# Attention, MoE and Sinkhorn MoE on one core: plain first block, four-quarter mixing, later column sums, an earlier check of decays, own room for raw pair inputs

## The chip, the cores and the metric

One Trainium2 chip, one core. The metric is the device time of one execution of the whole program, in microseconds (us).

## The reference

Three layers follow one another, all in fp32. The weights of the first MoE come as float64 words.

```python
f = 1.0 / (1.0 + np.exp(-f_logit))            # B 4, H 8, S 768, D 48
for t in range(S):
    state = f[:, :, t, :, None] * state + np.einsum('bhd,bhe->bhde', k[:, :, t], v[:, :, t])
    y[:, :, t] = np.einsum('bhd,bhde->bhe', q[:, :, t], state)
...
h = x @ w_in; r = np.maximum(h, 0.0); x = (r * r) @ w_out   # 3072 tokens, 384 -> 2048 -> 384
...
logits = x @ w_gate                                          # 8 experts
P = np.exp(logits - logits.max())
for _ in range(8):
    P /= P.sum(1, keepdims=True) + 1e-09
    P /= P.sum(0, keepdims=True) + 1e-09
    P *= N / E
for e in range(E):
    out += P[:, e:e + 1] * (np.maximum(x @ w1[e], 0.0) @ w2[e])   # 384 -> 1024 -> 384
```

## The kernel before, in words

**Order of the work.** Nothing is ordered by hand. `Plan` (from line 66) holds each piece of work as a step with an engine, an estimated length, a due time, the steps it needs and a lag (extra time until its result counts as there). `Plan.order` lists them as a list scheduler does, the step with the earliest due time first among those that are ready, and the program issues them in that list. On the chip each engine runs its instructions in that fixed order and waits where an input is not there: what is queued behind waits too.

**Attention.** The 3072 tokens are 24 chunks `c` of 128, six to a sequence. A chunk gets decays by scans on VectorE (`sg`, `minf` keeps the smallest), products of k and q with decays (`kq`), masked products among its tokens (`Psb`), and a state (`Sh`) from the chunks before it. `mix` (functions `new_y`, `mix_pair`, `mix`) makes y of a chunk on TensorE: four pairs p of heads, each head j of the pair in a half of y's partitions. Per pair there are two products with `Psb` (128 rows, 64 columns each, line 383) and, if the sequence has a state, two with the state (48 rows, 64 columns, line 386) into the same tile. Then `y_part` copies y as two rounded halves for the fast products: `hi` on ACT (step `yh`), the rest on VectorE (`yl`).

**First MoE.** Blocks `j` of 384 tokens (8 of them, three chunks each) by 16 weight tiles `f`; step i = 16 j + f. e1(i) (line 499) makes 9 products of 128x128 weights by 384 columns: for each third of the width w_hi x_hi, w_hi x_lo and w_lo x_hi. ACT makes relu, square and `hi`, VectorE `lo` (line 515), and e2(i) (line 525) 9 products into three accumulators. The weights are read as float64 words while the first block runs. A tile n goes through ACT (`cva`, `cvw`), VectorE (`cvb`: clamp line 937, fields 941, sign 945), POOL (`cvs`: sum, 949), then ACT (`cvh`: w_hi, line 280) and VectorE or POOL (`cvl`: w_lo, line 283). Which of the two, `LO_DVE` says: ten tiles on VectorE, six on POOL. e1(f) of the first block needs `cvl`(f). Attention chunks and these steps are interleaved by the plan. `keep_warm` (line 245) puts idle products of 128 columns on TensorE where the plan sees a gap near the start.

**Gates.** Logits `L` are collected, then 8 Sinkhorn iterations: row sums and scaling on VectorE (`skr`), column sums as a product with ones on TensorE (`skt`, line 989, tile `csum`), column scaling on VectorE (`skc`, from line 993). `pt` turns the result around. They run beside the first phases of the second MoE.

**Second MoE.** Three pairs p of 2 x 512 tokens, 8 experts; an e-phase is 66 products of 512 columns (line 678) for two steps, in products called p1, p2, p6, p5, p3, p7, p22, p4 that use sums of the inputs, and an o-phase is 72 products (line 729). ACT copies (line 696), VectorE adds (700, 705) and squares up hidden values (718), VectorE weighs o by the gate (752) and POOL accumulates (761). For each pair the inputs x are loaded (`ldx`, by SP's queue, in a ring `rawp` that the raw weights use too), summed (`xs`, VectorE) and split (`xhi` on ACT, `xlo` on VectorE). For p of 1 and 2 these wait for p4 of the step before, and p1 waits for all of them.

**Check of decays.** `in_range` takes the smallest decay of a row on VectorE and the maximum over partitions on POOL (`partition_all_reduce`, line 904); `choose` loads the flag into a register, and a slow path is taken after the program if it is set. The steps stand at `n1 + 200` and `n1 + 230` in the plan's time, in the second MoE.

## Time and profile before

| | us |
|---|---|
| time before, median of 3 runs (2130.74 to 2133.03) | 2131.81 |
| the profiled execution's own time | 2132.19 |
| its span in the trace | 2130.4 |
| TensorE busy | 2080.0 (98%) |
| VectorE busy | 1325.2 (62%) |
| ACT busy | 886.4 (42%) |
| POOL busy | 638.1 (30%) |

The span reaches from the first to the last instruction in the trace. Shares are of the span, over stages with different limits; the stages are read apart further down.

### The profile page before, as it was taken

How to read it: one execution, taken by the hardware profiler on the slowest of the kernel's cores; microseconds unless marked ns; L12 is line 12 of the kernel's file. 1: busy time of each engine (PE TensorE's matmuls, PEld its weight loads, DVE VectorE, ACT ScalarE, POOL GpSimd, SP SyncE). 2: the span in 40 equal slices, each digit the busy share in tenths (PEclk: the TensorE clock that was granted, in tenths of full speed). 3: DMA queues.
4: the chain of work that ended last, by engine and by line, in shares of the span. 5: the costliest groups of instructions: out<-in, count | busy, mean ns of one | idle time of the engine just before them, and what ended most of it. 6: DMA issues, size and time to landing. Idle time of an engine off the chain costs nothing.

```text
span 2130.4 us, 27837 instructions
## 1 busy us (share of the span) xinstructions
PE 2080.0 (98%) x10686; PEld 1762.8 (83%) x10686; DVE 1325.2 (62%) x2022; ACT 886.4 (42%) x1505; POOL 638.1 (30%) x636
## 2 busy tenths in 40 slices
PE   7889999999999999999999999999999999999998
PEld 5789899998987888878878888888887888888886
DVE  8973443332477666657677666756767766766674
ACT  4754444454643433423434433433433433443341
POOL 4531100010103333333332333334233243333331
PEclk9899999999999999999999999999999999999999
DMA  7342212110203111112122112121213111211210
GB/s 269 127 128 65 77 67 83 57 49 7 81 31 91 55 55 60 55 55 70 55 86 88 55 55 70 55 62 52 68 62 108 61 59 52 69 55 55 70 45 32
DMA packets 55114, 148.76 MB, mean 70 GB/s; under 512 B 6332, under 2 KB 15548, under 8 KB 54972
## 3 DMA queue, kind: packets, MB, share of 16 engines
q1 hardware_dynamic: 54972, 146.90, 21.6%
q8 instruction: 85, 1.39, 0.3%
q14 instruction: 57, 0.47, 0.1%
HBM read 135.28 MB, written 9.54 MB: 68 GB/s over the span
## 4 chain that ended last, share of the span: by engine, by line
PE 90%; DVE 6%; issue 1%; DMA 1%; POOL 1%; ACT 0%; SPq 0%; DVEq 0%; POOLq 0%; ACTq 0%
PE o L729 35%; PE e L678 33%; PE e L499 9%; PE a L525 8%; PE y L383 1%; PE y L386 1%; PE pp L344 1%; DVE cv_t L937 1%; DVE cv_t L945 1%; PE lg L540 1%; DVE lo L515 1%; PE ds L366 0%; DVE cv_t L941 0%; DVE w L283 0%; DVE sg L318 0%
## 5 line engine op out<-in xcount | busy, mean ns | idle before, releaser
L729 PE MATMUL o<-h,w 128*128 128x512 f32 x3456 | 792.8, 389 | 0.0
L729 PEld LDWEIGHTS o<-h,w 128*128 128x128 f32 x3456 | 648.1, 188 | 135.6 <-DVE sc L752 0.7
L678 PE MATMUL e<-x,w 128*128 128x512 f32 x3168 | 734.6, 391 | 10.4 <-DVE t L700 5.3
L678 PEld LDWEIGHTS e<-x,w 128*128 128x128 f32 x3168 | 597.2, 189 | 137.5 <-DVE t L700 7.0
L696 ACT COPY s<-e 128x512 f32<-128x512 f32 x288 | 168.9, 586 | 836.1 <-PE e L678 831.4
L761 POOL TENSOR_TENSOR acc<-acc,sc 128x512 f32<-128x512 f32 x258 | 334.4, 1303 | 536.4 <-DVE sc L752 529.5
L752 DVE TENSOR_TENSOR sc<-o,pb 128x512 f32<-128x512 f32 x264 | 182.0, 690 | 372.3 <-PE o L729 339.1
L718 DVE SCALAR_TENSOR_TENSOR h<-v,h 128x512 fp32r<-128x512 f32 x384 | 275.3, 736 | 1.8 <-ACT h L713 1.3
L713 ACT ACTIVATE h<-v 128x512 fp32r<-128x512 f32 x384 | 242.2, 631 | 52.8 <-DVE v L705 52.6
L705 DVE TENSOR_TENSOR v<-e,s 128x512 f32<-128x512 f32 x288 | 198.0, 688 | 74.7 <-ACT w L663 56.5
L650 POOL TENSOR_TENSOR rawa<-rawa 128x256 f32<-128x256 f32 x96 | 81.1, 845 | 537.4 <-DMA rawa<-in_wa_dram 347.8
L499 PE MATMUL e<-x,w 128*128 128x384 f32 x1152 | 229.0, 342 | 9.7 <-DVE w L283 6.2
L499 PEld LDWEIGHTS e<-x,w 128*128 128x128 f32 x1152 | 200.6, 190 | 16.7 <-DVE w L283 7.8
L515 DVE TENSOR_TENSOR lo<-g,hi 128x384 fp32r<-128x384 f32 x128 | 83.3, 653 | 208.6 <-ACT hi L511 208.6
L525 PE MATMUL a<-hi,w 128*128 128x384 f32 x768 | 200.1, 341 | 0.0
L667 DVE TENSOR_TENSOR w<-rawa,w 128x768 fp32r<-128x768 f32 x192 | 157.8, 823 | 8.1 <-ACT w L663 8.1
L663 ACT CAST w<-rawa 128x768 fp32r<-128x768 f32 x192 | 135.2, 728 | 29.6 <-DMA rawa<-in_wa_dram 12.4
L525 PE MATMUL a<-lo,w 128*128 128x384 f32 x384 | 131.0, 341 | 11.8 <-DVE lo L515 11.7
L525 PEld LDWEIGHTS a<-hi,w 128*128 128x128 f32 x768 | 140.3, 191 | 1.5 <-issue 0.3
L504 ACT ACTIVATE g<-e 128x384 f32<-128x384 f32 x128 | 62.9, 491 | 179.6 <-PE e L499 163.2
L328 POOL TENSOR_TENSOR kq<-kq,sg 128x512 f32<-128x512 f32 x24 | 30.9, 1287 | 290.7 <-DVE sg L318 161.6
L667 DVE TENSOR_TENSOR w<-rawc,w 128x768 fp32r<-128x768 f32 x96 | 92.5, 964 | 2.1 <-ACT w L663 2.0
(103 smaller groups left out, 1313.1 us busy)
## 6 DMA issues: line engine op xcount, KB each, us to landing
rawa<-in_wa_dram SPq DMA_DIRECT2D x96, 384.0 KB, 3.0
rawc<-in_wc_dram SPq DMA_DIRECT2D x96, 384.0 KB, 3.4
raw<-in_wm_dram SPq DMA_DIRECT2D x16, 768.0 KB, 6.2
pb<-ptd SPq DMA_DIRECT2D x24, 512.0 KB, 3.7
fraw<-in_fkq_dram SPq DMA_DIRECT2D x23, 512.0 KB, 4.0
...
```

The source lines that it names most:

```text
L499: pe.matmul(ps, w[:, wl, k * 128:(k + 1) * 128], xx[:, xl, k, :], start=n == 0, stop=n == 3 * KD - 1)
L525: pe.matmul(acc1[j][m], w[:, wl, D + m * 128:D + (m + 1) * 128], g, start=f == 0 and n == 0, stop=f == NF - 1 and n == 2)
L663: act.copy(out=W2[g, k][:, 0, 0:n], in_=src)
L667: dve.tensor_tensor(out=W2[g, k][:, 1, 0:n], in0=src, in1=W2[g, k][:, 0, 0:n].bitcast(F32), op=ALU.subtract)
L678: pe.matmul(ps, w[a], x[b], start=start and n == 0, stop=stop and n == 2, skip_group_check=True)
L696: act.copy(out=snap[g, n], in_=bank[g, "a"])
L705: dve.tensor_tensor(out=vs[g, k], in0=bank[g, k], in1=other, op=ALU.add)
L713: act.activation(out=hs[g // 2, t, f][:, 0], in_=vs[g, k], func=ACTF.Relu)
L718: dve.scalar_tensor_tensor(out=h[:, 1], in0=vs[g, k], scalar=0.0, in1=h[:, 0].bitcast(F32), op0=ALU.max, op1=ALU.subtract)
L729: pe.matmul(ob[q, t, m], w[:, a, c:c + 128], h[:, b], start=f == 0 and n == 0, stop=f == 3 and n == 2)
L752: dve.tensor_tensor(out=dst, in0=ob[q, t, m], in1=pbt[p, e][:, t * TB:(t + 1) * TB], op=ALU.mult)
L761: eng.tensor_tensor(out=acc[p, t, m], in0=acc[p, t, m], in1=sc[q, t, m], op=ALU.add)
```

## The change

- **Plain first block.** In block j = 0 e1 and e2 use plain fp32 products with the summed weight itself, tile `R`: three products for each of e1 and the three accumulators where there were nine. That block has no `hi`, no `lo` and no rounded halves of y. e1(f) needs `cvs`(f); `cvh` and `cvl` are due 16 steps later, all sixteen `cvl` on VectorE. The slots of `R` are used again for w tiles.
- **Quarters.** y of a chunk lies in two PSUM tiles, pair p in tile p % 2. Head j of pair p writes half j ^ (p & 1) of the partitions. Two pairs go together: their four products with `Psb`, then their four with the state. Weight rows are permuted in the host's layout to match. The copies of y are two instructions each; mix of a chunk needs `yl` of the chunk before.
- **Column sums.** The lag of `skr` is 2.8 instead of 0.8, so `skt` is listed later.
- **Check of decays.** It moves to `n1 - 12`, the last block of the first MoE, the flag's copy to POOL; `choose` needs the first o of super-step 14.
- **Raw inputs of pairs 1 and 2** get a pool of their own, are loaded earlier, summed and split earlier, each split behind the last product that reads its old tile; p1, p6 and p22 need only their own part.
- `dynamic_dma_scratch_size=1024` is set when the program is built.

```diff
-LO_DVE = (4, 6, 8, 9, 10, 11, 12, 13, 14, 15)
...
+    def cv_total(n):
+        R[n] = wb.tile([128, WCOL], F32, tag=f"b{n}", name="r")
+        F64(nc, cvt[n], raws[n]).total(R[n])
+
     def cv_hi(n):
-        act.copy(out=new_w(n)[:, 0, :], in_=cvt[n])
+        new_w(n)
+        act.copy(out=W[n][0], in_=R[n])

     def cv_lo(n):
-        (dve if n in LO_DVE else pool).tensor_tensor(out=W[n][:, 1, :], in0=cvt[n], in1=W[n][:, 0, :].bitcast(F32), op=ALU.subtract)
+        dve.tensor_tensor(out=W[n][1], in0=R[n], in1=W[n][0].bitcast(F32), op=ALU.subtract)
...
-        add(("cva", n), "act", 0.74, due, lambda n=n: cv_abs(n), [("ldw", n), if_(n >= 3, ("cvl", n - 3))], start=CV_AT + CV_STEP * n)
+        add(("cva", n), "act", 0.74, due, lambda n=n: cv_abs(n), [("ldw", n), if_(n >= 3, ("cvs", n - 3))], start=CV_AT + CV_STEP * n)
...
-        add(("cvh", n), "act", 0.74, due, lambda n=n: cv_hi(n), [("cvs", n), if_(n >= NF - 2, ("cvs", n - 4))])
-        add(("cvl", n), *(("dve", 0.88) if n in LO_DVE else ("pool", 1.78)), due, lambda n=n: cv_lo(n), [("cvh", n)])
+        add(("cvs", n), "pool", 1.9, due, lambda n=n: cv_total(n), [("cvb", n, 2), ("cvw", n)])
+        gone = [(s, k) for k in left_by(n) for s in ("e2", "cvl")] + ([("cvs", n - 4)] if n >= 14 else [])
+        add(("cvh", n), "act", 0.8, due + NF, lambda n=n: cv_hi(n), [("cvs", n)] + gone)
+        add(("cvl", n), "dve", 0.95, due + NF, lambda n=n: cv_lo(n), [("cvh", n)])
...
+    def y_at(c, p):
+        return tmp["y", c, p % 2], p // 2
+
+    def mix_in(c, p, rows=64):
+        vv, st = vt[c % 3], Sh.get(c)
+        y, n = y_at(c, p)
         for j in range(2):
-            h = 2 * p + j
-            pe.matmul(y[64 * j:64 * j + rows, p, :], vv[:, h * DH:h * DH + rows], Psb[c][:, j, p, :], start=True, stop=st is None)
...
+            h, o = 2 * p + j, 64 * (j ^ (p & 1))
+            pe.matmul(y[o:o + rows, n, :], vv[:, h * DH:h * DH + rows], Psb[c][:, j, p, :], start=True, stop=st is None)
+
+    def mix_state(c, p, rows=64):
+        kk, st = kq[c % 3], Sh.get(c)
+        y, n = y_at(c, p)
+        for j in range(2):
+            o = 64 * (j ^ (p & 1))
+            if st is not None:
+                pe.matmul(y[o:o + rows, n, :], st[64 * j:64 * j + DH, p, 0:rows], kk[64 * j:64 * j + DH, 1, p, :], start=False, stop=True)

     def mix(c):
         new_y(c)
-        for p in range(NP):
-            mix_pair(c, p)
+        for p in range(0, NP, 2):
+            for f in (mix_in, mix_state):
+                for i in range(2):
+                    f(c, p + i)
         Psb.pop(c)
...
+        if i < NF:
+            for k in range(KD):
+                pe.matmul(ps, R[i][:, k * 128:(k + 1) * 128], xx[:, 0, k, :], start=k == 0, stop=k == KD - 1)
+            return
...
+            if j == 0:
+                pe.matmul(acc1[j][m], R[f][:, D + m * 128:D + (m + 1) * 128], g, start=f == 0, stop=f == NF - 1)
+                continue
```

The lines on pairs, column sums and decays:

```diff
-        x2r[p, t] = rawp.tile([128, KD, TB], F32, tag="raw", name="xraw")
+        x2r[p, t] = pools["xr"].tile([128, KD, TB], F32, tag=f"x{t}", name="xraw") if p else rawp.tile([128, KD, TB], F32, tag="raw", name="xraw")
...
-            plan.load(("ldx", (p, t)), 786, u - 5.9 + 0.01 * t, lambda p=p, t=t: ldx(p, t),
-                      [("x2o", j, KD - 1) for j in js] + slot_of["x", (p, t)], n=len(js))
+            gone = slot_of["x", (0, t)] if p == 0 else ["right"] + [(s, p - 1, n) for s, n in (("xs", 3), ("xlo", 0), ("xlo", 1)) if p > 1]
+            plan.load(("ldx", (p, t)), 786, u - (9.0 if p else 5.9) + 0.01 * t, lambda p=p, t=t: ldx(p, t),
+                      [("x2o", j, KD - 1) for j in js] + gone, n=len(js))
         for n in range(4):
-            add(("xs", p, n), "dve", 0.69, u - 3.0 + 0.1 * n, lambda p=p, n=n: x_sum(p, n),
-                [("ldx", (p, 0)), ("ldx", (p, 1)), before, ("xs", p, n - 1) if n else None])
...
+            add(("xs", p, n), "dve", 0.69, u - (5.5 if p else 3.0) + 0.1 * n, lambda p=p, n=n: x_sum(p, n),
+                [("ldx", (p, 0)), ("ldx", (p, 1)), "left", ("xs", p, n - 1) if n else ("xlo", p - 1, 2) if p else None])
+
+        for i, (n, k, old) in enumerate(((0, 3, "p3"), (2, 4, "p7"), (1, 2, "p4"))):
+            d = u - (4.5 if p else 3.0) + 0.3 * i
...
-            needs["p1"] += [("xlo", p, n) for n in range(3)]
+            for name, n in (("p1", 0), ("p6", 2), ("p22", 1)):
+                needs[name] += [("xlo", p, n)]
...
-        add(("skr", it), "dve", 1.7, d, lambda: sk.rows(P), [done], lag=0.8)
+        add(("skr", it), "dve", 1.7, d, lambda: sk.rows(P), [done], lag=2.8)
...
+    def in_range_all():
         pool.partition_all_reduce(gmx, mx, 128, bass.bass_isa.ReduceOp.max)
-        dve.tensor_copy(out=flag, in_=gmx)
+        pool.tensor_copy(out=flag, in_=gmx)
...
-    add("range", "dve", 1.0, n1 + 200, in_range, ["P", ("o", 10, 1, 2)])
-    add("choose", "dve", 0.1, n1 + 230, choose, ["range", ("o", 14, 1, 2)])
+    add("range", "dve", 0.3, n1 - 12, in_range, [("scanf", NCH - 1)])
+    add("rangeall", "pool", 3.5, n1 - 11, in_range_all, ["range"])
+    add("choose", "dve", 0.6, n1 + 100, choose, ["rangeall", ("o", 14, 0, 0)])
```

VectorE's queue at the end of the first block, before: `w` is a `cvl`, `Psb` the masking of a chunk, `sg` to `d` the scans of the next chunk, and the two `lo` belong to steps 14 and 15; the next `lo` in the queue, three rows on, is that of step 16.

```order
L349 TENSOR_TENSOR Psb<-pp,mask 128x512
L283 TENSOR_TENSOR w<-cv_t,w 128x768
L349 TENSOR_TENSOR Psb<-pp,mask 128x512
L515 TENSOR_TENSOR lo<-g,hi 128x384
L324 SCALAR_TENSOR_TENSOR sg_125<-sg_125,d_126 128x516
L325 TENSOR_TENSOR minf<-minf,sg_125 128x4
L316 MEMSET sg_124 128x8
L317 MEMSET d_126 128x4
L318 SCALAR_TENSOR_TENSOR sg_124<-sg_124,d_126 128x516
L319 TENSOR_SCALAR d_126<-sg_124 128x4
L320 RECIPROCAL d_126<-d_126 128x4
L515 TENSOR_TENSOR lo<-g,hi 128x384
```

The same place with the change, from behind the last sign to the `lo` of step 16:

```order
L340 SCALAR_TENSOR_TENSOR sg_125<-sg_125,d_126 128x516
L341 TENSOR_TENSOR minf<-minf,sg_125 128x4
L298 TENSOR_TENSOR w<-r,w 128x768 x4
L332 MEMSET sg_124 128x8
L333 MEMSET d_126 128x4
L334 SCALAR_TENSOR_TENSOR sg_124<-sg_124,d_126 128x516
L335 TENSOR_SCALAR d_126<-sg_124 128x4
L336 RECIPROCAL d_126<-d_126 128x4
L340 SCALAR_TENSOR_TENSOR sg_124<-sg_124,d_126 128x516
L341 TENSOR_TENSOR minf<-minf,sg_124 128x4
L298 TENSOR_TENSOR w<-r,w 128x768 x5
L560 TENSOR_TENSOR lo<-g,hi 128x384
```

The `lo` of steps 14 and 15 are gone, nine `cvl` stand where one stood (a tenth a little earlier), and `Psb` comes behind the `lo` of step 16.

TensorE's queue at the mix of the last chunk, before: `a` are accumulators of the first MoE, `vt` the values, `kq` the queries; the last two rows stand there four times in all, once for each pair.

```order
L525 MATMUL a1_4404<-hi_4685,w_805 128x384 x2
L525 MATMUL a1_4404<-lo_4686,w_805 128x384
L525 MATMUL a2_4405<-hi_4685,w_805 128x384 x2
L525 MATMUL a2_4405<-lo_4686,w_805 128x384
L383 MATMUL y_4743<-Psb_4688,vt2_129 64x128 x2
L386 MATMUL y_4743<-kq2_123,Sh_4623 64x128 x2
```

The same mix with the change; the last four rows stand there twice:

```order
L573 MATMUL a2_4216<-lo_4503,w_799 128x384
L408 MATMUL y_4560<-Psb_4505,vt2_129 64x128 x2
L408 MATMUL y_4561<-Psb_4505,vt2_129 64x128 x2
L416 MATMUL y_4560<-kq2_123,Sh_4438 64x128 x2
L416 MATMUL y_4561<-kq2_123,Sh_4438 64x128 x2
```

The products with `Psb` of two pairs now stand together, and behind them the four with the state, into two tiles y.

TensorE's queue in the e-phase beside the Sinkhorn iterations, before: `csum` is a column sum, the e rows are products of the second MoE.

```order
L989 MATMUL csum<-sk_cs,sk_ones 128x8
L678 MATMUL e_5812<-x_5131,w_5341 128x512 x3
L678 MATMUL e_5812<-x_5131,w_5312 128x512 x3
L678 MATMUL e_5828<-x_5130,w_5406 128x512 x3
L678 MATMUL e_5832<-x_5130,w_5406 128x512 x6
L678 MATMUL e_5828<-x_5132,w_5583 128x512 x3
L989 MATMUL csum<-sk_cs,sk_ones 128x8
L678 MATMUL e_5852<-x_5132,w_5583 128x512 x3
L678 MATMUL e_5862<-x_5132,w_5406 128x512 x3
L678 MATMUL e_5862<-x_5130,w_5406 128x512 x3
L678 MATMUL e_5828<-x_5132,w_5583 128x512 x3
L989 MATMUL csum<-sk_cs,sk_ones 128x8 x2
```

Between two column sums with the change:

```order
L1047 MATMUL csum<-sk_cs,sk_ones 128x8
L730 MATMUL e_5599<-x_5040,w_5132 128x512 x3
L730 MATMUL e_5637<-x_5040,w_5145 128x512 x3
L730 MATMUL e_5637<-x_5040,w_5132 128x512 x3
L730 MATMUL e_5651<-x_4969,w_5268 128x512 x3
L730 MATMUL e_5655<-x_4969,w_5268 128x512 x6
L730 MATMUL e_5651<-x_4999,w_5412 128x512 x3
L730 MATMUL e_5674<-x_4999,w_5412 128x512 x3
L730 MATMUL e_5681<-x_4999,w_5268 128x512 x3
L730 MATMUL e_5681<-x_4969,w_5268 128x512 x3
L1047 MATMUL csum<-sk_cs,sk_ones 128x8
```

Where 18 and 12 products stood between column sums, 30 stand now.

## Rows read from the trace of the kernel before

**Rows 1.** Busy time by stretch: stretch, length, PE, PEld, DVE, ACT, POOL, PEclk, DMA, GB/s.

```profile
50.00:60.00 10.00, 6.97 (x43) 6.22 (x44) 9.86 (x15) 6.91 (x11) 5.52 (x3) 0.50 0.47 158
34.00:143.65 109.65, 86.80 (x541) 74.80 (x540) 106.45 (x127) 66.76 (x108) 60.70 (x35) 0.89 0.44 142
144.00:594.00 450.00, 449.90 (x3230) 416.67 (x3229) 172.80 (x321) 222.96 (x414) 45.12 (x39) 1.00 0.19 62
```

**Rows 2.** The chain that ended last: start, length, work; second MoE.

```profile
626.30 2.05 PE e L678 x9
...
652.59 16.65 PE o L729 x72
...
934.44 16.34 PE o L729 x72
...
971.04 16.38 PE o L729 x72
...
1131.10 16.32 PE o L729 x72
1147.42 14.96 PE e L678 x66
```

**Rows 3.** Timeline of DVE: start, length, engine, line, operation; two conversions.

```profile
59.73 0.55 DVE L937 TENSOR_SCALAR cv_t<-cv_t 128x768 f32<-128x768 f32 x1
...
61.78 0.95 DVE L283 TENSOR_TENSOR w<-cv_t,w 128x768 fp32r<-128x768 f32 x1
62.65 2.20 DVE L937 TENSOR_SCALAR cv_t<-cv_t 128x768 f32<-128x768 f32 x1
...
67.23 2.21 DVE L937 TENSOR_SCALAR cv_t<-cv_t 128x768 f32<-128x768 f32 x1
```

**Rows 4.** Timeline of POOL beside them; in brackets the idle time before.

```profile
61.99 2.44 POOL L949 TENSOR_TENSOR cv_t<-cv_t,raw 128x768 int32<-128x768 int32 x1 [2.60 <-issue]
64.39 1.51 POOL L331 TENSOR_TENSOR kq<-kq,sg 128x512 f32<-128x512 f32 x1
```

**Rows 5.** Timeline of DVE: the last sign, and lo of step 16.

```profile
126.11 0.96 DVE L945 SCALAR_TENSOR_TENSOR cv_t<-raw,cv_t 128x768 int32<-128x768 int32 x1
...
140.81 0.54 DVE L515 TENSOR_TENSOR lo<-g,hi 128x384 fp32r<-128x384 f32 x1
```

**Rows 6.** Timeline of PE: warm-up passes and what follows them.

```profile
37.54 2.62 PE L245 MATMUL warm<-shift 128*128 128x128 f32 x22
39.91 3.65 PE L499 MATMUL e<-x,w 128*128 128x384 f32 x18
```

**Rows 7.** Timeline of PE: the end of block 1; e1(18), then e2(16).

```profile
132.94 4.62 PE L499 MATMUL e<-x,w 128*128 128x384 f32 x16 [1.74 <-DVE w L283]
...
142.09 1.72 PE L499 MATMUL e<-x,w 128*128 128x384 f32 x9
143.65 0.51 PE L525 MATMUL a<-hi,w 128*128 128x384 f32 x2
```

**Rows 8.** Timeline of PE: the mix of chunk 7.

```profile
217.28 0.44 PE L383 MATMUL y<-Psb,vt 128*64 128x128 f32 x4
217.65 0.43 PE L386 MATMUL y<-kq,Sh 48*64 48x128 f32 x4
...
220.22 0.67 PE L366 MATMUL ds<-vt,Kn 128*64 128x48 f32 x16
```

**Rows 9.** Timeline of POOL: the reduction over partitions.

```profile
956.16 0.38 POOL L904 PARTITION_ALL_REDUCE gmx<-mx  x1 [5.96 <-issue]
```

**Rows 10.** Timeline of PE: start of the second pair.

```profile
1112.58 2.20 PE L678 MATMUL e<-x,w 128*128 128x512 f32 x9
1116.97 7.77 PE L678 MATMUL e<-x,w 128*128 128x512 f32 x33 [2.19 <-ACT s L696]
```

**Rows 11.** Timeline of PE: start of the third pair.

```profile
1616.73 2.20 PE L678 MATMUL e<-x,w 128*128 128x512 f32 x9
1621.25 14.83 PE L678 MATMUL e<-x,w 128*128 128x512 f32 x57 [2.32 <-ACT s L696]
```

125 lines of the change are left out of this document (69 added, 56 removed).

## The prediction

> **What bounds the kernel now.** I read the page first, then the busy time by stretches, then the chain of waits, and last the timelines of single engines where chain and stretches showed a loss. The profiled execution took 2132.19 us, 0.38 above the median of the runs shown (2131.81); the sum below is made against 2132.19. By the stretches [rows 1], TensorE is never idle in blocks 2 to 8 of the first MoE (144 to 594 us: 449.90 of 450), so there a removed pass of TensorE is worth its length. In block 1 (34 to 143.65) it is VectorE that is full: 106.45 of 109.65, with TensorE at 86.80. The reader should see that TensorE has 23 us to spare there, and that its clock was granted at 0.89 in that stretch and at 0.50 from 50 to 60, when the product waited for the conversion. The second MoE is a chain of e-phases and o-phases. An undisturbed e-phase lasts 14.96 [rows 2]; what a phase takes above that is loss.
>
> **Plain first block.** What VectorE does to convert a weight tile (clamp, fields, sign) takes 61.78 − 59.73 = 2.05 us when POOL is quiet; the next one, from 62.65 to 67.23, takes 4.58 [rows 3]. In between POOL ran two instructions, at 61.99 and 64.39 [rows 4]: so each of POOL's large elementwise instructions costs VectorE (4.58 − 2.05) / 2 = 1.26 us. A `cvl` costs VectorE 62.65 − 61.78 = 0.87 from start to start, though its own row says 0.95; a `lo` of 0.54 [rows 5] so costs about 0.48. Before the last sign of a conversion, which ends at 126.11 + 0.96 = 127.07 [rows 5], the change
> - removes 14 `lo`: 14 × 0.48 = 6.7;
> - takes 6 `cvl` off POOL: 6 × 1.26 = 7.6;
> - moves two of VectorE's eight `cvl` behind it: 2 × 0.87 = 1.7.
>
> The last sign then ends 16 us sooner, at 111. By the order ten `cvl` (8.7), two copies of x (about 1) and the scans of two chunks follow, and then `lo(16)`. Before, that `lo` came 140.81 − 127.07 = 13.7 behind the sign [rows 5]: scans, and two `cvl`, two `lo` and two `Psb`, each under 0.9: some 9.5 of it scans. So it comes at 111 + 8.7 + 1 + 9.5 = 130.2, and e2(16), which started at 143.65 [rows 7], behind it. TensorE has to be there by then. What plain products cost it: 22 warm-up passes of 128 columns lie between 37.54 and 39.91 [rows 6], 0.108 each, two passes to a product. A product of 384 columns is 6 × 0.108 = 0.646, a step of six products 3.88, where a step of 18 fast ones takes twice 143.65 − 142.09, or 3.12 [rows 7]: 16 × 0.76 = 12 us more. From 34 on TensorE then has 86.80 + 12, less 3 for the mixes of three chunks (below) and 3 for warm-ups that the order no longer has: 93, which ends at 127 if it never waits. The 23 us to spare so hide the 12; if the cover were smaller, TensorE would set the end. Before, its last wait was for the last `cvl`, up to 132.94 [rows 7]; now e1(15) needs the sum of its tile alone.
>
> VectorE's 130 and TensorE's 127 are close, so I take e2(16) at 130.6, **−13**. High end: 17 (127). Low end: 5, where the scans among the `cvl` are stretched by POOL and TensorE waits here and there for the first tiles. From ACT 16 `hi` go; it has 40 us to spare here.
>
> **Quarters.** The mix of one chunk is eight groups of four passes, from 217.28 to 220.22, 0.367 each [rows 8]. The two halves of a pair start together and take two passes and a switch: 0.367 = 2 × 0.108 + 0.151. The change puts two pairs side by side. The products with `Psb` (full height, half the columns) keep their number: four to a group, one switch, 4 × 0.108 + 0.151 = 0.58. The products with the state are 48 rows by 64 columns, a quarter of the array each. If the four quarters run at once, a group of eight instructions takes 0.367. A chunk is 2 × (0.58 + 0.367) = 1.89 instead of 2.94: 1.05 saved. If only two run at once the group takes 0.58 and the chunk 2.32: 0.62 saved. Of the chunks with a state, 15 lie where TensorE is never idle (7 to 11, 13 to 17, 19 to 23): 15.7 or 9.3 us. The trace shows two row halves at once (that pace), and never four quarters. The state's group already has both row halves at work [rows 8], so I take **−15.7** and keep 9.3 as the low end. The y copies become two instructions on ACT and VectorE where one was, and the next chunk's mix waits for y only through `yl`; both engines have half their time free [rows 1], so I price that at 0.
>
> The Trainium skill, "TensorEngine Tiling (Array Packing)", Restrictions and Gotchas, speaks against it: different row tiles cannot access the same PSUM bank simultaneously. In the old group as in the new one, both row halves of a pair write one y tile, and the old one ran at 0.367, not at 4 × 0.108 + 0.151. What the rule would give stands among the rivals.
>
> **Column sums later.** The e-phase that starts at 626.30 ends at 652.59: 26.29 us, 11.3 above 14.96 [rows 2]. Five column sums stand in it: TensorE reaches each before VectorE has the row sums, and queued behind are the e products, for which the next steps of VectorE wait. By the order three stay in it, and the rest follow later. If the loss went with the number, two fifths of 11.3 = 4.5 would go. But the chain of the eight iterations gets later by it, and the first o-phase's scaling needs the end of that chain: next late are the accumulators of o. I take **−2**, between 0 and 6.
>
> **Range of decays.** From the end of an o-phase at 934.44 + 16.34 = 950.78 to the next at 971.04 are 20.26 us [rows 2], 5.3 above 14.96. POOL's all-reduce stands there, with 5.96 us ahead of it in which POOL waits for nothing shown [rows 9]: no accumulation runs meanwhile, the buffers of o stay taken, and TensorE waits. The change puts it into the last block of the first MoE, where POOL is 10% busy [rows 1] and TensorE takes nothing from it: hidden. The flag's copy goes to POOL's queue, and only the late `choose` waits for it. I take **−5.3** (low end 4.0: `choose` still waits at a border).
>
> **Raw inputs of a pair.** At the second pair TensorE starts its first nine products at 1112.58, stands 2.19 us, and the o-phase begins at 1131.10: 18.52, so 3.6 lost [rows 2, 10]. At the third, 1616.73 to 1621.25 + 14.83 = 1636.08: 19.35, 4.4 lost, again with the halt after the first nine [rows 11]. VectorE and ACT make the sums and halves of x there, after the last p4, ahead of what p2 and p6 need. The change loads x nine of the plan's steps ahead (5.9 before) into room of its own (SP issues it; the weight loads queued behind it no longer share its slots), forms the sums 5.5 ahead, and each half behind the last product that used it; p1 waits for its own alone. Of 8.0 lost I take **−5.5**; one `xlo` of about 1 us still falls between VectorE's steps at each border. Ends: 1 and 7.8.
>
> **The sum.** 13 + 15.7 + 2 + 5.3 + 5.5 = 41.5; 2132.2 − 41.5 = **2090.7** us. All low ends together are 5 + 9.3 + 0 + 4 + 1 = 19.3 (2113), all high ones 17 + 15.7 + 6 + 5.3 + 7.8 = 51.8 (2080).
>
> **Rivals.**
> - Two quarters at a time: the mix saves 0.62, and the time is 2090.7 + 6.4 = 2097. For it: no row shows more than two at once. Against it: nothing in the pace of the old groups is taken by waiting.
> - Row halves of one bank take turns: a state group of eight passes, two columns at once, would be 8 × 0.108 + 0.151 = 1.0, a chunk 2 × (0.58 + 1.0) = 3.16, 0.22 more than now on 15 chunks: 2090.7 + 15.7 + 3.3 = 2109.7. Against it stand the old groups of 0.367 with both row halves in one y tile [rows 8].
> - The first block gains nothing, because the ten `cvl` with the scans between them now stand ahead of `lo(16)` and take what was freed: 2103.7.
> - Block 1 goes as fast as TensorE can, 17 us: 2086.7. It needs the scans and `cvl` to be quick once POOL is quiet.
> - **Slower**: plain products at half clock. The clock was 0.50 where TensorE stood waiting for the conversion [rows 1]. A step at half clock is 7.75; sixteen are 124, and the other work of TensorE up to 144 is about 86.80 − 16 × 3.12 = 37: from 34 on that ends at 195 instead of 143.65, 51 later. 2132.2 + 51 − 28.5 (the other four terms) = 2155. It decides once the plain steps run at 0.61 of full speed on the mean (34 + 62 / 0.61 + 37 is 29 above 143.65); the 0.89 of the whole stretch [rows 1], and waits that get shorter, speak against it.
> - That the conversion is not lightened can be excluded: the order shows the 16 `lo` gone from VectorE and six `cvl` from POOL.
>
> **Chances.** Forecast 0.56 (its own range 2083 to 2100), two quarters 0.15, block 1 as fast as TensorE 0.11, first block without gain 0.10, turns in a bank 0.05, half clock 0.03. I give 2078 to 2110 as the range: it leaves out the half clock, half of the turns in a bank, and tails of the others. About 0.2% (4.3 us) can be told from no change. Only the half clock is slower: 0.03; 0.02 lies within 0.2%, for several low ends with a new wait at a border; faster 0.95.
>
> **What would show it.** In the changed kernel e2(16) should start near 131, with VectorE still full to about 110, the conversion of a tile taking 2.05 us with POOL quiet, and a plain step 3.9. A mix of a late chunk should take 1.9 us (2.3: two quarters; above 2.9: turns), with the starts of all four state products within some ns. The all-reduce should stand in POOL before 594, no o-phase near 950 should follow an e-phase of 20, and the two pairs' e-phases should be near 16. The prediction is wrong if the e-phase with the column sums gets longer than 26.3, if TensorE now waits for `cvl` in block 2, or if the clock falls under 0.8 in block 1.

## The result, and the profile after

The changed kernel took 2105.14 us (median of 4 runs, 2102.58 to 2107.77), the kernel before 2132.42 beside it; the ratio is 0.9873, 95% interval 0.9856 to 0.9890. That is 27.3 us faster, where 41.5 were forecast: the time lies in the range, a good third of the gain is missing. The profiled execution took 2106.62 us, 25.6 less than the one of before.

First lines of the page of the changed kernel: the span, and busy time by engine.

```profile
span 2104.9 us, 27580 instructions
...
PE 2064.0 (98%) x10558; PEld 1734.1 (82%) x10558; DVE 1314.3 (62%) x2029; ACT 878.9 (42%) x1513; POOL 629.3 (30%) x631
```

TensorE works 16 us less, and the rest of the gain (25.5 us of span) is idle time that went. The program is a row of stages, so the difference can be read off one mark after the other. The marks are the start of e2(16), of the first and the fourth e-phase of the second MoE (e-phase 1 and 4), of e-phases 11, 15 and 34, all by the timeline of TensorE, and the last addition on VectorE.

| stretch | before | after | forecast | measured |
|---|---|---|---|---|
| start to e2(16): plain first block | 143.65 | 138.16 | −13 | −5.5 |
| to e-phase 1: mixes of blocks 2 to 8 | 443.71 | 428.54 | −15.7 | −15.2 |
| e-phase 1 to 4: column sums | 112.99 | 115.79 | −2 | +2.8 |
| 4 to 11: no change there | 218.96 | 218.96 | 0 | 0 |
| 11 to 15: range of decays | 130.50 | 125.15 | −5.3 | −5.35 |
| 15 to 34: both borders of pairs | 602.43 | 601.77 | −5.5 | −0.7 |
| 34 to the last addition, and from there to the end | 478.1 | 476.5 | 0 | −1.6 |

Busy time by stretch of the changed kernel (columns as in [rows 1]): two stretches ahead of block 1, block 1, a tenth of it, and the blocks where TensorE is full.

```profile
14.00:18.00 4.00, 4.00 (x20) 2.33 (x19) 3.83 (x9) 0.89 (x2) 0.00 (x0) 0.50 1.01 413
18.00:22.00 4.00, 4.00 (x27) 3.15 (x26) 0.82 (x3) 1.07 (x3) 1.19 (x1) 0.50 1.01 406
...
34.00:138.16 104.16, 89.58 (x452) 54.54 (x453) 99.13 (x122) 62.27 (x100) 52.08 (x30) 0.95 0.46 157
...
115.00:125.00 10.00, 6.49 (x17) 3.69 (x18) 9.85 (x12) 4.29 (x8) 6.47 (x5) 0.91 0.24 60
144.00:560.00 416.00, 416.00 (x3120) 393.47 (x3119) 170.99 (x332) 211.55 (x410) 45.89 (x38) 1.00 0.20 64
```

The plain products did not lose the clock: 0.95 over the block, against 0.89 [rows 1]. But TensorE still has 14.6 us idle there, 3.5 of it from 115 to 125, near the end. And ahead of the block, from 14 to 22 us, TensorE is busy without a gap at half clock, 1.2 GHz: experiment 3 shows what that was worth.

**Block 1.** The marks on VectorE came near where they were forecast, those on TensorE did not. Timeline of VectorE: the last sign (it ends at 111.86; forecast 111) and `lo(16)` (forecast 130.2).

```profile
110.90 0.96 DVE L1003 SCALAR_TENSOR_TENSOR cv_t<-raw,cv_t 128x768 int32<-128x768 int32 x1
...
132.88 0.55 DVE L560 TENSOR_TENSOR lo<-g,hi 128x384 fp32r<-128x384 f32 x1
```

Timeline of TensorE at the plain e1 of steps 13, 14 and 15, and of ACT beside it: `w<-r` is the rounded half of a tile (`cvh`), `g<-e` the relu of a step.

```profile
109.78 2.17 PE L540 MATMUL e<-x,r 128*128 128x384 f32 x6 [1.19 <-ACT g L549]
...
115.23 2.17 PE L540 MATMUL e<-x,r 128*128 128x384 f32 x6 [1.34 <-ACT g L549]
...
122.62 3.53 PE L540 MATMUL e<-x,r 128*128 128x384 f32 x6 [3.28 <-ACT g L549]
```

```profile
113.86 0.83 ACT L295 CAST w<-r 128x768 fp32r<-128x768 f32 x1 [2.95 <-POOL r L1007]
114.60 0.48 ACT L549 ACTIVATE g<-e 128x384 f32<-128x384 f32 x1
...
121.25 0.83 ACT L295 CAST w<-r 128x768 fp32r<-128x768 f32 x1 [4.89 <-DVE w L298]
121.99 0.48 ACT L549 ACTIVATE g<-e 128x384 f32<-128x384 f32 x1
```

Three plain products, six passes, take 1.94 (104.55 to 106.49 in the same timeline; forecast 3.88 for the two halves of a step). But ACT stands 2.95 us for POOL's sum of a tile, and 4.89 us for a `cvl` on VectorE in whose place the new tile goes. The relu queued behind is late, and TensorE waits for it, last 3.28 us ahead of e1(15); that one then runs 3.53, with the granted clock at 0.57 from 123 to 127 us. So e1(15) starts only at 122.6. A further halt shows in the waits of TensorE in this block (columns: total, times, longest):

```profile
PE e L540 <- ACT g L549: 5.8, 3, 3.3
PE pp L360 <- DVE x L453: 5.5, 1, 5.5
```

`pp` waits for the copy of y: y now takes both PSUM tiles that it shares with `pp`, where it took one.

**Mix.** Timeline of TensorE, the mix of a chunk (before: [rows 8]).

```profile
210.29 0.62 PE L408 MATMUL y<-Psb,vt 128*64 128x128 f32 x8
210.84 0.45 PE L416 MATMUL y<-kq,Sh 48*64 48x128 f32 x8
211.22 0.66 PE L408 MATMUL y<-Psb,vt 128*64 128x128 f32 x8
...
212.19 1.83 PE L544 MATMUL e<-x,w 128*128 128x384 f32 x9
```

1.90 us from 210.29 to 212.19, forecast 1.89. The state group takes 0.38 (210.84 to 211.22), and its first four products start within 20 ns.

**Sinkhorn stretch.** The e-phase with the column sums got shorter, as meant: the second e-phase took 26.21 us before (626.14 to 652.35) and takes 20.26 now (605.36 to 625.62). But the iterations that left it now stand in the second o-phase, ahead of VectorE's squares `h` and of its additions to the accumulators, and TensorE waits for both. Timeline of TensorE, the second o-phase before, then parts of it now:

```profile
652.35 16.89 PE L729 MATMUL o<-h,w 128*128 128x512 f32 x72
```

```profile
629.92 0.73 PE L781 MATMUL o<-h,w 128*128 128x512 f32 x2 [1.73 <-DVE h L770]
...
635.98 3.01 PE L781 MATMUL o<-h,w 128*128 128x512 f32 x12 [2.37 <-DVE acc L798]
```

It lasts 22.56 (625.62 to 648.18) instead of 16.72. And the chain of eight iterations ends later, so that what hangs on it (the transposed gates, their way through memory, POOL's scaling of the accumulators) falls on the third e-phase. Before, in POOL's timeline, then now with the third e-phase of TensorE and VectorE beside it:

```profile
662.20 5.75 POOL L755 TENSOR_TENSOR acc<-acc,pb 128x512 f32<-128x512 f32 x4 [1.68 <-DVE w L667]
```

```profile
652.56 10.60 POOL L807 TENSOR_TENSOR acc<-acc,pb 128x512 f32<-128x512 f32 x6 [9.50 <-DMA pb<-ptd]
```

```profile
658.28 2.05 DVE L719 TENSOR_TENSOR w<-rawc,w 128x768 fp32r<-128x768 f32 x1
660.25 1.77 DVE L770 SCALAR_TENSOR_TENSOR h<-v,h 128x512 fp32r<-128x512 f32 x1
```

```profile
648.18 13.08 PE L730 MATMUL e<-x,w 128*128 128x512 f32 x57
663.28 2.34 PE L730 MATMUL e<-x,w 128*128 128x512 f32 x9 [2.01 <-DVE t L752]
```

Before, the scaling stood beside the o-phase of 652.59 [rows 2]. Now it stands beside an e-phase: VectorE's weight half takes 2.05 and a square 1.77 instead of 0.95 and 0.68, and TensorE waits 2.01. The third e-phase takes 2.3 us more than before (17.28, from 648.18 to 665.46) and the o-phase behind it 0.7. In all 6.0 were gained and 8.9 lost.

**Borders.** Timeline of TensorE at the second pair: the o-phase ahead of it, the e-phase from 1091.04, and the next o-phase.

```profile
1072.84 2.43 PE L781 MATMUL o<-h,w 128*128 128x512 f32 x10
1076.00 3.48 PE L781 MATMUL o<-h,w 128*128 128x512 f32 x14 [0.74 <-DVE h L770]
1080.01 11.20 PE L781 MATMUL o<-h,w 128*128 128x512 f32 x48 [0.52 <-DVE sc L804]
1091.04 5.60 PE L730 MATMUL e<-x,w 128*128 128x512 f32 x24
1098.31 9.82 PE L730 MATMUL e<-x,w 128*128 128x512 f32 x42 [1.67 <-DVE t L752]
1107.97 16.56 PE L781 MATMUL o<-h,w 128*128 128x512 f32 x72
```

The halt after the first nine products [rows 10] is gone, and three others came, in the o-phase before it and in the e-phase. VectorE's timeline names them:

```profile
1077.07 2.29 DVE L681 TENSOR_TENSOR x<-xs,x 128x2048 fp32r<-128x2048 f32 x1
1079.27 0.68 DVE L804 TENSOR_TENSOR sc<-o,pb 128x512 f32<-128x512 f32 x1
...
1093.00 0.77 DVE L671 TENSOR_TENSOR xs<-xraw 128x512 f32<-128x512 f32 x1 [3.71 <-DMA xraw<-x2d]
```

An `xlo` of 2.29 us stands ahead of a weighing (`sc`); and the sums for the third pair, some 490 us early, wait 3.71 us for their transfer with a weighing and an addition of the e-phase behind them. Summed over all phases from e-phase 15 to 34, the e-phases lost 7.6 us above 14.96 before and lose 2.0 now, and the o-phases lost 0.5 above 16.32 before and lose 5.5 now: the gain in the e-phases went into the o-phases.

### The profile page after: what moved, and what is told of

Same layout as the page of the kernel before. It is cut to its first block, busy times and chain, and to the rows that moved or that the text cites. A ratio compares the mean times of both kernels' runs of the same rounds, so it can differ in the third digit from the quotient of the medians.

```text
span 2104.9 us, 27580 instructions
## 1 busy us (share of the span) xinstructions
PE 2064.0 (98%) x10558; PEld 1734.1 (82%) x10558; DVE 1314.3 (62%) x2029; ACT 878.9 (42%) x1513; POOL 629.3 (30%) x631
## 4 chain that ended last, share of the span: by engine, by line
PE 89%; DVE 6%; POOL 1%; DMA 1%; issue 1%; ACT 0%; DVEq 0%; POOLq 0%; SPq 0%; ACTq 0%
PE o L781 36%; PE e L730 32%; PE e L544 9%; PE a L573 8%; PE pp L360 1%; PE y L408 1%; PE lg L588 1%; DVE cv_t L1003 1%; DVE cv_t L999 1%; DVE cv_t L995 1%; DVE h L770 1%; DVE w L298 1%; PE y L416 1%; DVE v L757 1%; DVE sg L334 0%
## 5 line engine op out<-in xcount | busy, mean ns | idle before, releaser
L730 PEld LDWEIGHTS e<-x,w 128*128 128x128 f32 x3168 | 595.2, 188 | 132.2 <-DVE t L752 8.9
L544 PE MATMUL e<-x,w 128*128 128x384 f32 x1008 | 198.1, 340 | 0.0
L560 DVE TENSOR_TENSOR lo<-g,hi 128x384 fp32r<-128x384 f32 x112 | 65.7, 586 | 203.0 <-ACT hi L556 202.4
L544 PEld LDWEIGHTS e<-x,w 128*128 128x128 f32 x1008 | 174.0, 188 | 4.8 <-issue 2.4
L573 PE MATMUL a<-hi,w 128*128 128x384 f32 x672 | 171.7, 336 | 0.0
L573 PEld LDWEIGHTS a<-hi,w 128*128 128x128 f32 x672 | 120.5, 188 | 0.9
L573 PE MATMUL a<-lo,w 128*128 128x384 f32 x336 | 112.4, 335 | 0.0
```

The source lines that it names most:

```text
L544: pe.matmul(ps, w[wl][:, k * 128:(k + 1) * 128], xx[:, xl, k, :], start=n == 0, stop=n == 3 * KD - 1)
L573: pe.matmul(acc1[j][m], W[f][wl][:, D + m * 128:D + (m + 1) * 128], g, start=f == 0 and n == 0, stop=f == NF - 1 and n == 2)
L730: pe.matmul(ps, w[a], x[b], start=start and n == 0, stop=stop and n == 2, skip_group_check=True)
```

## The experiments

All changed lines are against the changed kernel (2105.14 us), unless said otherwise; each was timed against the kernel before, in 4 runs.

**1. The lag alone.**

```diff
-        add(("skr", it), "dve", 1.7, d, lambda: sk.rows(P), [done], lag=2.8)
+        add(("skr", it), "dve", 1.7, d, lambda: sk.rows(P), [done], lag=0.8)
```

> The changed kernel (2105.1 us) with the lag of the row sums back at 0.8, all else as changed. Theory: the later column sums end the Sinkhorn chain later, so POOL's six scalings of accumulators fall on the third e-phase and stretch VectorE there (the changed kernel lost 2.8 us between the first e-phase and the fourth against the kernel before); with 0.8 the scalings fall into the o-phase again and the stretch from the start of the first e-phase to that of the fourth, 115.95 us in the changed kernel and 113.16 before, comes back to 113 to 114, the time to about 2102. Rival: the loss comes from the four sums of x of the second pair, which now stand in that stretch; then taking the lag back loses what the lag gained, the stretch is 117 to 119 and the time 2106 to 2108.

Measured 2100.88 us (0.9854, 0.9837 to 0.9870). The stretch from e-phase 1 to 4 is 679.92 − 567.98 = 111.94. POOL's scaling runs from 640.52 on, the o-phase from 632.18 to 648.64:

```profile
632.18 16.62 PE L781 MATMUL o<-h,w 128*128 128x512 f32 x72
648.64 15.12 PE L730 MATMUL e<-x,w 128*128 128x512 f32 x66
```

```profile
640.52 6.21 POOL L807 TENSOR_TENSOR acc<-acc,pb 128x512 f32<-128x512 f32 x4
```

The theory holds for the stretch: it took 111.9 to 114.4 us in all five runs with lag 0.8, and 115.6 to 120.9 in the changed kernel and the seven others with 2.8; between these two profiles the difference is 3.85. But POOL's scaling is the smaller part of the cause: the second o-phase takes 16.46 here (632.18 to 648.64) and 22.56 in the changed kernel. The whole gained 4.3, though with intervals that overlap.

**2. ACT's halves held.**

```diff
-        gone = [(s, k) for k in left_by(n) for s in ("e2", "cvl")] + ([("cvs", n - 4)] if n >= 14 else [])
+        gone = [(s, k) for k in left_by(n) for s in ("e2", "cvl")] + ([("cvs", n - 4)] if n >= 14 else []) + ([("sq", NF - 1)] if n >= 11 else [])
```

> The changed kernel with the rounded halves of tiles 11 to 15 on ACT (cvh) held until the square of step 15 is done. Theory: in block 1 of the changed kernel ACT stood 2.95 and 4.89 us in front of such a half (for POOL's sum of tile 15, and for a cvl on VectorE whose slot it takes), with the relu of steps 13 and 14 queued behind, and TensorE waited 5.8 us for them and then ran at a lower clock; without that e1(15) starts at 116 to 117 instead of 122.6 and e2(16) at 130 to 133 instead of 138.2, the time falls by 5 to 8 us to 2097 to 2100. Rival: VectorE's queue sets the place anyway; lo(16) starts at 132.9 as before, e2(16) not before 136, and the gain is under 2 us.

Measured 2099.90 us (0.9852, 0.9835 to 0.9868). Timeline of TensorE:

```profile
113.62 2.10 PE L540 MATMUL e<-x,r 128*128 128x384 f32 x6
...
127.38 0.51 PE L573 MATMUL a<-hi,w 128*128 128x384 f32 x2
```

e1(15) starts at 113.62 without a wait and e2(16) at 127.38, 10.8 sooner than in the profiled run of the changed kernel. Of that, 6.5 is the queue of ACT (133.9, the mark of run 3, less 127.4) and 4.3 goes with the clock ahead of the block (run 3). The interval of the time overlaps that of the changed kernel's; the mark is the clearer sign. The halt of 5.5 us for the copy of y is still there in this run; runs 8 and 9, with 3.9 and 5.5 us of halts ahead of `pp`, end the block at 127.07 and 127.14, so there is no sign that the end hangs on it. The forecast's mark (130.6) was there to be had; the halves in ACT's queue had taken it.

**3. The sums of x held.** `xs` of a later pair waits for p1 two steps before it.

```diff
-                [("ldx", (p, 0)), ("ldx", (p, 1)), "left", ("xs", p, n - 1) if n else ("xlo", p - 1, 2) if p else None])
+                [("ldx", (p, 0)), ("ldx", (p, 1)), ("p1", p * NE * NST - 2) if p else "left", ("xs", p, n - 1) if n else ("xlo", p - 1, 2) if p else None])
```

> The changed kernel with the sums of x of the second and third pair (xs) held until two steps before their pair. Theory: the plan had pulled them to the first place where their data were due, those of the second pair into the Sinkhorn stretch (595 to 603 us) and those of the third to 1093, where VectorE stood 3.71 us for a transfer, with an o weighing and an e addition behind it; TensorE lost 1.67 us there. Held, the second pair's border loses about 1.7 to 2.5 us less, the stretch with the Sinkhorn iterations 0 to 2.8 less: 2100.5 to 2103.5. Rival: the border's loss is the three xlo (1.75, 2.29 and 1.22 us) between h and weighing, and the sums now fall there too: no gain or up to 2 us slower.

Measured 2107.43 us (0.9890, 0.9873 to 0.9906). The halt of 1.67 went; the waits of TensorE from 690 us on are now

```profile
PE o L781 <- DVE sc L804: 4.8, 4, 1.5
```

and the stretch from e-phase 15 to 34 is 604.1 (601.8), which is the rival's side, though within what this stretch varies by with nothing changed in it (600.6 to 604.5 us in seven runs). The Sinkhorn stretch stayed at 115.89, so the early sums had no part in it.

e2(16) came at 133.90, 4.3 sooner than in the changed kernel, though nothing was changed in block 1. From about 30 us on each of VectorE's conversions starts 4.2 sooner, up to the last sign (106.66, where it was 110.90); the difference arises before. Busy time by stretch of this run, then the timeline of TensorE at the products `pp` of the second chunk, here and in the changed kernel, and VectorE's first step behind them there:

```profile
14.00:18.00 4.00, 4.00 (x40) 2.70 (x38) 3.79 (x10) 1.80 (x5) 0.25 (x1) 1.00 1.02 416
18.00:22.00 4.00, 3.71 (x42) 2.74 (x38) 3.88 (x7) 2.18 (x5) 2.11 (x2) 1.00 1.01 407
```

```profile
16.98 1.16 PE L360 MATMUL pp<-kq 48*128 48x128 f32 x16
```

```profile
19.37 2.08 PE L360 MATMUL pp<-kq 48*128 48x128 f32 x16
```

```profile
21.48 1.29 DVE L365 TENSOR_TENSOR Psb<-pp,mask 128x512 f32<-128x512 f32 x2 [3.14 <-PE pp L360]
```

The clock is at full speed from 14 us on, as it was in the profiled execution of the kernel before; in that of the changed kernel the same row of products ran at half of it to 22 us, and VectorE, which is full in block 1, stood 3.14 us for them and never made it up. No run changes this clock alone. But the profiles with the changed kernel's first block fall into two groups: e2(16) came at 132.95 to 133.90 at full clock from 14 us on (runs 3, 4, 6 and 11), at 138.16 and 139.44 at half of it (the changed kernel and run 1).

**4. Two quarters.** The place of a pair's half in y, with the rows of the weights put to match.

```diff
-            h, o = 2 * p + j, 64 * (j ^ (p & 1))
+            h, o = 2 * p + j, 64 * j
...
-            o = 64 * (j ^ (p & 1))
+            o = 64 * j
...
```

> The changed kernel with head j of every pair in half j of y (no exchange for odd pairs, rows of the weights permuted to match): the four state products of two pairs then use only two quarters of the array, two products to each. Theory (four quarters at once were the gain): the state group takes 0.58 us instead of 0.38, a mix 2.3 instead of 1.90, and 15 mixes beside a full TensorE cost 6 us: 2111. Rival: the gain came from fewer changes between the kinds of product alone, not from the quarters: the mix stays at 1.9 and the time at 2105.

Measured 2109.85 us (0.9906, 0.9889 to 0.9922). The state group of the same mix:

```profile
207.38 0.65 PE L416 MATMUL y<-kq,Sh 48*64 48x128 f32 x8
207.97 0.66 PE L408 MATMUL y<-Psb,vt 128*64 128x128 f32 x8
```

It takes 0.59 instead of 0.38, a mix 2.31, and the blocks 2 to 8 434.65 us instead of 428.54: 6.1 for the quarters, forecast 6.4. That leaves 9.1 of the 15.2 for the grouping in fours, which was not undone by itself.

**5. yl of chunk 3 earlier.** Due 6 steps lower in block 1; the last scan of chunk 5 and the clamp of tile 6 wait for it.

```diff
-            at("yl", "dve", 0.62, 3, lambda c: y_part(c, 1), [("yh", c)])
+            at("yl", "dve", 0.62, 3 if blk > 1 else -3, lambda c: y_part(c, 1), [("yh", c)])
...
-        at("scanf", "dve", 0.75, -2, scan_f, [("scanr", c), ("sig", c)])
+        at("scanf", "dve", 0.75, -2, scan_f, [("scanr", c), ("sig", c), ("yl", 3) if c == 5 else None])
...
-        add(("cvb", n, 0), "dve", 0.6, due, lambda p=part: p("clamp"), [("cva", n)])
+        add(("cvb", n, 0), "dve", 0.6, due, lambda p=part: p("clamp"), [("cva", n), ("yl", 3) if n == 6 else None])
```

> The changed kernel with the rest of y of chunk 3 (yl, VectorE) put earlier in VectorE's queue: its due time is lower in block 1, and the last scan of chunk 5 and the clamp of tile 6 wait for it in the plan. Theory: y now holds both PSUM tiles that the masked products share, so TensorE's next products of q and k wait for yl (5.5 us at 67 us in the changed kernel, 1.2 before), and the clock falls behind that halt; put earlier, the wait is under 2 us and the clock from 65 to 75 stays above 0.9. The end of block 1 is set later, by ACT's queue, so e2(16) comes only 0 to 3 us sooner: 2102 to 2105. Rival: the halt carries through to the end: e2(16) 5 us or more sooner, 2100 or less.

Measured 2105.53 us (0.9883, 0.9864 to 0.9902). The wait of 5.5 us is gone, but a halt of 4.1 that nothing in the profile accounts for stands ahead of a later `pp`, and e2(16) starts at 135.71, 2.5 sooner. That is not shown to come from the edit: the clock from 14 to 18 us was 0.85 in this execution and 0.50 in the changed kernel's.

**6. xlo and xs in the o-phases.**

```diff
-            add(("xlo", p, n), "dve", 0.16 + 0.53 * k, d, lambda p=p, n=n: x_lo(p, n), [("xhi", p, n)])
+            add(("xlo", p, n), "dve", 0.16 + 0.53 * k, d + (2.5 if p else 0.0), lambda p=p, n=n: x_lo(p, n), [("xhi", p, n)])
```

and `xs` held as in 3, for `("p4", p * NE * NST - 3)`.

> The changed kernel with the rest of x of a pair (xlo, VectorE) due 2.5 steps later, so that it stands in the gaps between the weighings of the last o-phase, and the sums of x held until the e-phase one super-step earlier is over, so that they stand in that o-phase. Theory: what is left of the loss at the two borders of pairs (3.9 us at the second in the changed kernel, 2.6 at the third, above undisturbed phases) is VectorE's order: 5.3 us of xlo ahead of h and of weighings, and the sums of the next pair in an e-phase; placed in gaps, each border loses under 1 us and the time falls by 4 to 5 us to 2100. Rival: the transfers and weight halves on ACT and POOL hold the borders too, and the loss stays above 2 us at each.

Measured 2105.80 us (0.9884, 0.9863 to 0.9905): inconclusive on the time. From e-phase 15 to 18 (second border) it took 95.57 instead of 97.77, from 30 to 34 (third) 128.94 instead of 127.75. The Sinkhorn stretch took 120.89 at a mean granted clock of 0.94, where run 3, with sums held in much the same way, had 115.89 at 0.99. Busy time by stretch, first the changed kernel, then this one:

```profile
560.00:620.00 60.00, 58.19 (x281) 49.48 (x279) 43.65 (x97) 26.79 (x46) 4.12 (x7) 1.00 0.20 63
620.00:690.00 70.00, 61.72 (x267) 49.49 (x268) 49.17 (x83) 23.13 (x38) 25.96 (x24) 0.98 0.23 70
```

```profile
560.00:620.00 60.00, 56.36 (x256) 46.81 (x255) 42.78 (x96) 24.66 (x41) 3.02 (x6) 0.96 0.18 57
620.00:690.00 70.00, 63.28 (x263) 50.66 (x262) 46.78 (x77) 22.07 (x37) 24.88 (x24) 0.93 0.23 70
```

**7. Six cvl on POOL.**

```diff
+LO_POOL = (0, 1, 2, 3, 5, 7)
...
-        dve.tensor_tensor(out=W[n][1], in0=R[n], in1=W[n][0].bitcast(F32), op=ALU.subtract)
+        (pool if n in LO_POOL else dve).tensor_tensor(out=W[n][1], in0=R[n], in1=W[n][0].bitcast(F32), op=ALU.subtract)
...
-        add(("cvl", n), "dve", 0.95, due + NF, lambda n=n: cv_lo(n), [("cvh", n)])
+        add(("cvl", n), *(("pool", 1.78) if n in LO_POOL else ("dve", 0.95)), due + NF, lambda n=n: cv_lo(n), [("cvh", n)])
```

> The changed kernel with six of the sixteen cvl (tiles 0, 1, 2, 3, 5 and 7) on POOL, as many as before the change. Theory (each large instruction of POOL costs VectorE 1.26 us, a cvl on VectorE 0.87): the last sign moves by 6 x 1.26 less the same cvl on VectorE that stood ahead of it, 5.2: some 2 us later; e2(16) 2 to 5 us later, as ACT's later halves wait for the slots that POOL leaves at 2.1 us a piece; 2107 to 2110. Rival: VectorE is no longer what sets the block, and taking work off it gains: e2(16) sooner, 2103 or less.

Measured 2118.96 us (0.9933, 0.9909 to 0.9956), worse than expected: e2(16) at 144.24, TensorE waiting 9.2 us for y and 5.7 for a relu in the block, and the Sinkhorn stretch at 120.92, at 0.94 of the clock as in run 6: 5.1 us more than in the changed kernel, in a stretch that the edit leaves as it was. The mark is 6.1 behind the changed kernel and 10.3 behind run 3, with a clock ahead of the block between theirs (0.81 from 14 to 18 us). From the fifth sign to the last (starts) VectorE takes 69.1 us where the changed kernel and run 3 both take 57.2. Clamp and fields take 9.6 more there, from start to start, with eight more instructions of POOL beside them (the six `cvl` and two products `kq`), 1.2 each, close to the 1.26 of the prediction; the scans of one more chunk now stand ahead of the last sign, and two `cvl` fewer.

**8. Four repairs at once** (1, 2, 5 and 6).

> The changed kernel with lag 0.8, the halves of tiles 11 to 15 held until step 15, yl of chunk 3 earlier, and xlo and xs of pairs in the o-phases. The four places lie one behind the other, so the gains should add: the block before e2(16) ends at 124 to 128 us (133.9 to 138.2 in the changed kernel's runs), the first to the fourth e-phase takes 112 (115.8), the borders lose 4 us less. From 2105.1: 7 to 10, 3.8 and 4 less, and up to 3 given back at the end of the program, where the kernel with lag 0.8 took 3 us longer: 2088 to 2093. Rival: the clock of block 1 falls again when TensorE is less loaded, and the sum of the gains stays under 10 us (2095 or more).

Measured 2095.08 us (0.9828, 0.9809 to 0.9846), the rival's side by a hair. e2(16) came at 127.07, in the range of the theory; e-phase 1 to 4 took 114.38, 1.4 less and not 3.8, in part because the first e-phase took 23.4 us at 0.93 of the clock where run 1 had 21.8 at 1.00; 15 to 34 took 601.4, 0.4 less and not 4; the end gave 2 us back.

**9. Repairs 1 and 2 alone.**

> The changed kernel with lag 0.8 and the halves of tiles 11 to 15 held until step 15, nothing else. Theory: the two repairs stand in different stages and add: e2(16) at 127 to 128, 112 us from the first to the fourth e-phase, the borders of pairs as in the changed kernel (601.8 from the fifteenth e-phase to the thirty-fourth); it does without what the earlier run with four repairs changed at the borders, which brought nothing there and cost 2.4 us in the Sinkhorn stretch: 2091 to 2094. Rival: the stretch of 111.9 with lag 0.8 was one lucky placing, and the clock falls there again: 114 or more, 2095 or more.

Measured 2097.91 us (0.9837, 0.9821 to 0.9854): e2(16) 127.14, e-phase 1 to 4 113.01, but 604.5 from 15 to 34. The two add up in their own stages; the time misses the theory, as the borders differ by 3 us with nothing changed there. The Sinkhorn stretch is 1.4 shorter than in run 8, but the first e-phase alone, at full clock here, is 1.6 shorter: a price of run 8's held sums is not shown.

**10. xlo in pieces.** As 9, each `xlo` of a later pair cut into pieces of 512 columns, due 2.5 later.

```diff
...
+                for a in range(k):
+                    add(("xlo", p, n, a), "dve", 0.69, d + 2.5, lambda p=p, n=n, a=a: x_lo(p, n, a, a + 1), [("xhi", p, n)])
...
```

> As the kernel before it in this call (lag 0.8, halves held), with every xlo of the second and third pair cut into pieces of 512 columns and due 2.5 steps later. Theory: what the borders still lose is one VectorE instruction of up to 2.29 us (3.38 with POOL beside it) in front of a weighing, for which the two o buffers are too few; pieces of 0.6 us between the weighings lose under 1 us a border, and the stretch from the fifteenth e-phase to the thirty-fourth falls from 601.8 to 597 to 599: 2088 to 2091. Rival: the weight halves that VectorE and ACT make in the same gaps hold the weighings as well, and the stretch stays above 600.

Measured 2094.38 us (0.9822, 0.9806 to 0.9839), the best median; it is not to be told from run 8. The stretch from 15 to 34 is 602.6, so its theory fell: the e-phases there lose nothing above 14.96, the o-phases 8.3.

**11. Range of decays back.**

```diff
-    add("rangeall", "pool", 3.5, n1 - 11, in_range_all, ["range"])
+    add("rangeall", "pool", 3.5, n1 + 200, in_range_all, ["range", "P", ("o", 10, 1, 2)])
```

> The changed kernel with POOL's all-reduce of the decays and the flag's copy back at its old place in the second MoE (behind the second half of the o of super-step 10), the reduction on VectorE left early. Theory: the 5.3 us lie in POOL's queue at the all-reduce alone: the stretch from the eleventh to the fifteenth e-phase, 125.15 us in the changed kernel and 130.5 before, is 130 to 131 again, the time 2110. Rival: they came from VectorE's two instructions or from the copy of the flag behind them; then the stretch stays under 127 and the time at 2106.

Measured 2110.21 us (0.9902, 0.9885 to 0.9918); 130.52 from e-phase 11 to 15, and POOL's timeline has the old halt:

```profile
936.27 0.38 POOL L961 PARTITION_ALL_REDUCE gmx<-mx  x1 [5.89 <-issue]
```

The 5.3 us belong to the two instructions on POOL, as the one on VectorE stayed early. The profiled execution is only 1.7 us longer than the changed kernel's, as its first block was 4.4 shorter (the clock was at full speed from 14 us on, e2(16) started at 133.80); its Sinkhorn stretch, where nothing was changed, took 118.16 at 0.96 of the clock.

**12. Two pieces between weighings.** As 10; each two pieces wait for the next weighing.

```diff
+                    at_ev = ((0, 3, 7)[i] + a) // 2
...
+                        [("xhi", p, n), ("ev", p * NE * NST // 2 - 1, at_ev // KD, at_ev % KD)])
```

> As the run with pieces of xlo (lag 0.8, halves of tiles 11 to 15 held, xlo of the second and third pair in pieces of 512 columns), with at most two pieces between two weighings of the last o-phase: each pair of pieces waits for the next weighing. Theory: at the borders TensorE waited for weighings alone (3.3 us in that run) because the plan, which is ahead of VectorE there, let three pieces stand in front of one; with the order forced, those waits fall under 1 us and the stretch from the fifteenth e-phase to the thirty-fourth goes from 602.6 to 598 to 600, the time from 2094.4 to 2090 to 2092. Rival: the first weighing is late from the work of the e-phase before it, and pieces in any order push the rest: the waits stay above 2 us, the time at 2094.

Measured 2098.44 us (0.9843, 0.9827 to 0.9860). The waits for weighings fell from 3.3 to 1.9, those for h rose from 1.4 to 3.0 with one of 1.0 for ACT, and 15 to 34 took 604.8. Neither theory explains the borders.

## Why the prediction was right or wrong

The time lies in the stated range (2078 to 2110) and above the forecast's own (2083 to 2100). It is nearest to the rival "the first block gains nothing" (2103.7), but that is chance: the block did gain, and the column sums and the pairs did not.

**Plain first block: right in kind, 7.5 us too much, for two reasons.** 4.2 of them go with the half clock from 14 to 22 us, ahead of the block, and are no part of the change: runs 3, 4, 6 and 11, which have its first block too, were at full clock from 14 on, and e2(16) came at 133.0 to 133.9, a gain of 9.8 or a little more. I did not see that the mark hangs on that clock. The other 3.3 are the step "TensorE has to be there by then": I summed TensorE's work and found 127, and of ACT only wrote that 16 `hi` go. The change also put `cvh` later (16 of them start between 40.7 and 123.8 us, the last six from 108.4 on), some of them behind a `cvl` or a sum that is not yet done and ahead of relus in ACT's queue. Run 2 takes that away for the last five tiles and reaches 127.38, what the rival "as fast as TensorE can" said (127).

Two sizes were off as well, and hid behind the clock: in run 3, at full clock, the last sign ends at 107.6, 19.4 sooner and not 16, and the agreement of the changed kernel's 111.86 with my 111 came of the lost 4.2. The rows of before, up to the last sign, show where the 3.4 lie (columns: busy us, mean ns):

```profile
L515 DVE TENSOR_TENSOR lo<-g,hi 128x384 fp32r<-128x384 f32 x14 | 13.5, 982 | 0.0
```

I had priced a `lo` by one row of 0.54. Ten of the 14 took that, and four, which began early in a sum on POOL, 1.87 to 2.23, so that `lo` took 13.5 us of VectorE where I took 6.7. The other way, clamp, fields and sign of the 16 tiles took 50.7 us before and 44.9 in the changed kernel: 5.8 less, where I took 7.6 for the `cvl` off POOL. The rest is not split up. The copies of y "priced at 0" were wrong too, 5.5 us of halt, though runs 8 and 9 give no sign that the end of the block hangs on it.

**Quarters: right.** 15.2 of 15.7, a mix of 1.90, and run 4 gives the price of two quarters as forecast. The sentence of the Trainium skill ("TensorEngine Tiling (Array Packing)", Restrictions and Gotchas) would have made a mix 3.16: here both row halves write one y tile in the same 20 ns, so the trace speaks against it for these shapes.

**Column sums later: wrong in sign.** The e-phase with the sums lost 6.0 us less, more than the 4.5 that counting them gave. The step that failed is the price of what is late next: I named the accumulators of o and left 2.5 for them (4.5 − 2), and it was 8.9, of which 5.8 lie in the second o-phase, for the iterations that moved there, and 3.0 in the two phases behind it, where POOL's scaling now falls. That o-phase takes 22.5 to 24.2 in all runs with lag 2.8 and 16.5 to 16.7 with 0.8.

**Range: right** to 0.1, shown by run 11.

**Pairs: −0.7 for −5.5.** The halt that I read was removed, and the e-phases gained what I forecast: 5.7 us less lost, with the two of the pairs at 16.93 and 14.96, near the 16 that I named. What failed is the price of what follows, "one `xlo` of about 1 us" at each border: the o-phases lose 5.0 us more. The three `xlo` take 1.75, 2.29 and 1.22, they all come in the first half of the o-phase, where each weighing frees a buffer of o, and the due times I read as dates only rank steps that are ready: the sums ran in the first gap of the plan. What would free the borders stays open: runs 3, 6, 10 and 12 moved the waits from weighing to h and back, with 600.0 to 604.8 us from e-phase 15 to 34, and seven runs with the changed kernel's border had 600.6 to 604.5. So neither those four nor the −0.7 itself can be told from that spread.

The end: from the last addition to the end of the span 7.35 us before, 5.26 after. It is 2 us longer again in the runs with lag 0.8. Why was not tried. None of the rivals came true as a whole.
